# Attention and gated feed-forward in one kernel: load and turn order of batch 1, order of two attention products, and the place of the second scores in chunks 3 to 6

## Chip, cores and metric

The kernel runs on one core of a Trainium2 chip. The metric is the device time of one execution in microseconds (us); the profile is one execution taken by the hardware profiler.

## What is computed

Eight batches of 576 tokens with 8 heads of 64 go through windowed attention. Heads 0 to 3 ("plain") see the last 32 tokens, heads 4 to 7 ("dilated") every fourth of the last 128. The result is the input of a gated feed-forward block.

```python
scores = scale * np.matmul(q, k.transpose(0, 1, 3, 2))
mask_plain = (rel >= 0) & (rel < window)                                      # window 32
mask_dil = (rel >= 0) & (rel < window * dilation) & (rel % dilation == 0)      # dilation 4
attn = np.exp(scores - max); attn = attn / (np.sum(attn) + 1e-09)
x = np.matmul(attn, v)            # turned to (4608 tokens, 512)
g = x @ w_gate                    # 512 x 1536
out = (0.5 * g * (1.0 + erf(g * inv_sqrt2)) * (x @ w_val)) @ w_out   # 1536 x 512
```

## The kernel before

The 4608 tokens are worked through in nine chunks of 512 for the feed-forward part. A chunk c has a gate stage (96 wide matmuls, 128x512, L611: 12 blocks, each with a gate and a value product over 4 parts of the inner dimension) and an out stage (48 wide matmuls, L618: 4 token blocks over 12 parts). Attention of batch c + 1 is put between the wide matmuls of chunk c's out stage; batch 0 comes ahead of the first chunk. The attention result is kept turned in `xT`, four tiles of 128 rows; the dilated heads fill two of them, the plain heads two.

The order is written out by hand. `run_program` reads a string of words: a number n pops n wide matmuls from the stage's list, and a letter with a number n is one step of a pair of heads n. Pairs 4 to 7 are batch 1: 4 and 5 plain, 6 and 7 dilated. In chunk c of the later ones, i and j are the first two pairs of batch c + 1 and k and l the second two. What follows @ is a place in PSUM. The steps are

- t: turn eight rows at a time of q or k on the tensor engine (L366) and copy the result out of PSUM (`turn_first`; pairs 12 and 14 are q, 13 and 15 are k); y: turn rows of nine, q and k together (L386, `turn_second`). The dilated heads of batch 1 use the rows of eight, the plain heads the rows of nine;
- S: scores (L446); P: their exponential on ACT (L476); M: times the mask on VectorE (L481);
- D: sums of the exponentials over the window, by a product with ones (L446, `P,ones` in the profile); l, r: logarithm (L573) and exponential of its negative (L579) on ACT, which give the inverse;
- N: exponentials times the values (L446, `P,v`); X: N times the inverse, on VectorE, into `xT` (L602);
- g, u: gelu on ACT (L770) and its product with the value part on VectorE (L775); w, e: an output block out of PSUM by VectorE (L631) or ACT (L629) and its store; E and G: load of ACT's table for exp/log or for gelu; V: `second` or `second_v`; F, H, R: loads and turns of a later batch.

PSUM has eight banks of 512 fp32; `ps` is one tile over all of them. The instructions of an engine run in the order in which they are written here; waits between engines follow from the data and the banks that they share.

Batch 1 has loads of its own, issued by GpSimd in `second` with a cast to fp16: rows of eight into the unused tails of `xT[2]` and `xT[3]` (72 partitions), rows of nine into `s16` (64 partitions). Ahead of them in GpSimd's queue stand the last gate and value weights (`load_w(3)`), behind them the three pieces of the output weights (`wo`), the masks and batch 1's dilated values. SP's loads of the plain values of batch 1 are held until the first piece of `wo` has landed. For later batches SP loads into `stage`, GpSimd casts, and SP's transposing DMAs turn q and k; the values are cast by GpSimd at L248.

Of the kernel before, what the change touches and what calls it, by code (L numbers as in the profile page):

```python
# [21 lines left out]
def kernel(  # L22
# [11 lines left out]
    B, H, S, D = q.shape  # L34
    NT, DM = out.shape
    DFF = moe_w_gate.shape[1]
    P = 128
# [64 lines left out]
    def eight(b):  # L102

        tails = [xT[2 * b + t][0:R8, 2 * S : 2 * S + HK * 8 * D] for t in range(2)]
        return [t.rearrange("p (h r d) -> p h r d", h=HK, r=8) for t in tails]
# [42 lines left out]
    def load_w(*parts):  # L148

        for i in parts:  # L150
            for t, w in ((wg_t, moe_w_gate), (wv_t, moe_w_val)):
                src = w[:, WC[i][0] : WC[i][1]].rearrange("(kc p) n -> p kc n", p=P)
                nc.gpsimd.dma_start(out=t[i], in_=src)

    def load_wo(i):
        return nc.gpsimd.dma_start(
            out=wo_t[i], in_=moe_w_out[i * CH : (i + 1) * CH, :].rearrange("(fc p) m -> p fc m", p=P)
        )
# [9 lines left out]
    def rows_in(src, r):  # L168

        return src.rearrange("h (p r) d -> p h (r d)", r=r)  # L170

    def load_eights(b, pairs=((0, HK),)):
        for h0, h1 in pairs:
            for t, src in zip(eight(b), (q, k)):
                rows_ = src[b, HK + h0 : HK + h1, :, :].rearrange("h (p r) d -> p h (r d)", r=8)
                nc.gpsimd.dma_start(out=t[:, h0:h1].rearrange("p h r d -> p h (r d)"), in_=rows_)

    def views(b):

        halves = [qraw[b % 2][:, t * QK : (t + 1) * QK] for t in range(2)]  # L180
        qp, kp = (t[:, 0:1280].rearrange("p (g c) -> p g c", g=2) for t in halves)
        qd, kd = (t[:, 1280:QK].rearrange("p (g r i) -> p g r i", g=2, r=4) for t in halves)
        vp, vd = (vraw[b % 3][:, a : a + 2 * NB2 * D].rearrange("p (e d) -> p e d", d=D) for a in (0, 2 * NB2 * D))
        return qp, qd, kp, kd, vp, vd
# [43 lines left out]
    def load_v(b, i, plain):  # L228

        st = st_of(i)  # L230
        for g in range(2 * plain):
            for x in range(2):
                rows_ = v[b, 2 * g + x].rearrange("(j p) d -> p j d", p=64)
                dst = st[half_of(x, b and g), 576 * g : 576 * g + 576].rearrange("p (j d) -> p j d", j=NB2)
                gated(nc.sync.dma_start(out=dst, in_=rows_))  # L235
        for g in range(2 - 2 * plain):
            for x in range(2):
                half = st[half_of(x, g), 576 * g : 576 * g + 512]
                rows_ = v[b, HK + 2 * g + x, 0 : 4 * P].rearrange("(i p r) d -> p i (r d)", i=2, r=4)
                nc.sync.dma_start(out=half.rearrange("p (i c) -> p i c", i=2), in_=rows_)  # L240
        for x in range(2 - 2 * plain):
            dst = st[half_of(x), 512:1152].rearrange("p (g c) -> p g c", c=64)[:, 0:10:9]
            heads = slice(HK + 1, HK + 3) if x else slice(HK, HK + 4, 3)
            nc.sync.dma_start(out=dst, in_=v[b, heads, S - 64 : S].rearrange("g p d -> p g d"))
# [51 lines left out]
    def v_cast(b, g, rest=False):  # L296

        dst = views(b)[5][:, NB2 * g : NB2 * g + NB2]
        for x in range(2):
            half = half_of(x, b and g)  # L300
            nc.gpsimd.dma_start(
                out=dst[half, 0:8].rearrange("p (i r) d -> p i (r d)", r=4),
                in_=v[b, HK + 2 * g + x, 0 : 4 * P].rearrange("(i p r) d -> p i (r d)", i=2, r=4),
            )
            if rest:
                heads = slice(HK + x, H, 2)
                if b:
                    heads = slice(HK + 1, HK + 3) if x else slice(HK, HK + 4, 3)
                nc.gpsimd.dma_start(
                    out=views(b)[5][half_of(x), NB2 - 1 : 2 * NB2 : NB2],  # L310
                    in_=v[b, heads, S - 64 : S].rearrange("g p d -> p g d"),
                )
# [9 lines left out]
    def two_masks():  # L322
        for x in range(2):
            half = slice(64 * x, 64 * x + 64)
            band1 = band[half, 64 * x : 64 * x + BQ]
            nc.gpsimd.tensor_copy(
                two_p[half, 0 : 8 * BQ].rearrange("p (j c) -> p j c", j=8),
                bass.AP(tensor=band1.tensor, offset=band1.offset, ap=[band1.ap[0], [0, 8], [1, BQ]]),
            )
            nc.gpsimd.tensor_copy(two_p[half, 8 * BQ : LP], band1[:, 0:BK])  # L330
        for r in range(4):
            nc.gpsimd.tensor_copy(two_d[:, 176 * r : 176 * r + BQ], two_p[:, 0:BQ])
            nc.gpsimd.tensor_copy(two_d[:, 176 * r + BQ : 176 * r + 176], two_p[:, 0:80])
        rest_mask(nc.gpsimd, two_d[:, LD - BK : LD])
# [339 lines left out]
    for h in range(0, HK, 2):  # L674
        for t, src, eng in ((0, q, nc.sync), (1, k, nc.scalar)):
            first = eng.dma_start(out=first_p[:, t, h : h + 2], in_=rows_in(src[0, h : h + 2], 6))
# [23 lines left out]
    def second():  # L700

        load_w(3)
        load_eights(1)
        for src, t in zip((q, k), nine):
            nc.gpsimd.dma_start(out=t.rearrange("p h r d -> p h (r d)"), in_=rows_in(src[1, 0:HK], 9))
        wo = [load_wo(i) for i in range(3)]
        two_masks()
        v_cast(1, 0, True)
        v_cast(1, 1)
        tiles["two", 1] = views(1)  # L710
        gate["dma"] = wo[0]
        load_v(1, 1, True)
        gate["dma"] = wo[2]
# [84 lines left out]
    def gate_words(c):  # L798

        if c == 0:  # L800
            return (
                "c0@0 c1@0 t0@0@1 t1@1@0 b1@6 W1@3@0 S0@4 P0 t4@0@1 W1@3@0 c2@0 c3@0 t5@1@0 t2@2@1 t3@3@0 D0@40 T0 B0 "
                "t6@1@1 W10@7 t7@0@0 S1@6 P1 b2@2 S2@2 P2 D1@60 T1 B1 b3@0 S3@0 P3 D2@20 A2 N0@40 X0 D3@00 N2@60 X2 A3 N3@20 1 "
                "N1@00 X1 X3 G V 15 g0 u0 g1 u1 4 g2 4 g3 4 u2 4 u3 4 g4 4 g5 4 u4 4 u5 4 g6 4 g7 4 u6 4 u7 4 g8 4 g9 4 u8 3 "
                "t12@4@1 t14@6@0 t13@5@1 t15@7@0 1 u9 8 g10 u10 1 y0@4@5 y1@6@7 7 g11 u11"
            )
        loads = {1: "F3", 2: "R", 3: "F5 H5", 4: "F6 H6", 5: "F7 H7"}.get(c, "")
        rest = " ".join(f"4 g{nb} 4 u{nb}" for nb in range(2, NNB - 1))
        if c == 1:
            return f"{loads} 8 G 3 g0 1 u0 3 g1 1 u1 {rest} 4 g{NNB - 1} 4"  # L810
        before = f"e3@{c - 1}" if c < NCH - 1 else ""
        return f"{before} {loads} 7 G 3 g0 1 u0 1 g1 4 u1 {rest} 4 g{NNB - 1} 4" + (f" u{NNB - 1}" if c > 6 else "")

    def out_words(c):

        if c == 0:
            return (
                "V1 F2 S6@4+S7@6 1 E P6 11 P7 1 M6 S4@4+S5@6 M7 1 P4 6 P5 M4 2 D6@40+D7@60 l6 l7 M5 r6 r7 6 w2@0 4 w1@0 4 "
                "w0@0 H2 D4@52+D5@22 N6@50+N7@20 X6 l5 X7 l4 r4 r5 10 N4@20+N5@40 X4 X5 2 e3@0"
            )  # L820
        if c > 6:
            return "12 e0 12 e1 12 e2 12 w3" if c < NCH - 1 else "12 e0 12 e1 12 e2 L"
        i, j, k, l = (NHP * (c + 1) + n for n in range(NHP))
        first = f"1 u11 4 S{i}@1+S{j}@4 E P{i} P{j} M{i} M{j} 7 w0 5" if c < 3 else f"E P{i} P{j} 1 u11 M{i} M{j} 12 w0 2"
        after = f"S{l + 1}@12+S{l + 2}@15" if 1 < c < 6 else ""
        return (
            f"{first} S{k}@1+S{l}@4 D{i}@11+D{j}@41 P{k} P{l} M{k} M{l} "
            f"{7 if c < 3 else 10} w1 l{i} l{j} r{i} r{j} {10 if c < 3 else 4} N{i}@10+N{j}@40 D{k}@12+D{l}@42 X{i} X{j} "
            f"{2 if c < 3 else 8} w2 {f'l{k} l{l} r{k} r{l}' if c < 3 else f'l{k} r{k} l{l} r{l}'} {8 if c < 3 else 6} N{k}@13+N{l}@43 {after} X{k} X{l} {4 if c < 3 else 5}"
        )  # L830

# [8 lines left out]
    def run_chunk(c):  # L840

        banks = out_banks(c)
        run_program(c, gate_words(c), gate_list(c), banks)
        run_program(c, out_words(c), out_list(c, banks), banks)
# [31 lines left out]
```

## Time and profile before

| | |
|---|---|
| median of 3 runs | 329.22 us (327.46 to 330.02) |
| the profiled execution | 328.32 us |
| its span, first to last instruction | 326.6 us |
| granted TensorE clock | 1.00 |
| instructions | 7737 |
| wide matmuls, L611 and L618 | 1284, mean 0.38 us as recorded |
| GpSimd's software DMA queue | 7.67 MB, 16.7% of 16 engines' span |
| SP's and ACT's DMA queue | 38.29 MB, 50.1% |

PE is the tensor engine, PEld its weight loads, DVE is VectorE, ACT is ScalarE, POOL is GpSimd, SP the engine that issues most DMAs. Busy times are sums of recorded durations; a wide matmul is recorded with 0.38 us, but they overlap, so distances between starts say how fast they follow one another. In a line of the timeline stand start, time from its first start to its last end, engine, line of the kernel, operation, output and inputs, shape and count; in brackets how long the engine had been idle and what ended it. "issue" means that nothing which the profile shows ended the wait.

### The profile page before, as it was taken

To read this page: it belongs to the slowest core of one execution; us is meant where nothing else is said; L and a number is where in the kernel's file an instruction comes from. 1 tells how busy PE (TensorE), PEld (TensorE's weight loads), DVE (VectorE), ACT (ScalarE), POOL (GpSimd) and SP (SyncE) were. 2 spreads that over 40 slices of the span, in tenths; PEclk is the share of its full clock that TensorE was granted. 3 is DMA by queue.
4 is the path that set the end of the run, shared out by engine and by line. 5 is a ranking of instruction groups with operands and counts; after the bars stand their busy time and mean duration, and the time that the engine had idled before them with its cause. 6 is when DMAs were issued, how large, how long until landed. Compare 5 with 4: busy or idle time off the path is not lost.

```text
span 326.6 us, 7737 instructions
## 1 busy us (share of the span) xinstructions
PE 320.2 (98%) x3207; PEld 156.5 (48%) x3207; DVE 151.4 (46%) x226; ACT 159.6 (49%) x240; POOL 82.2 (25%) x134
## 2 busy tenths in 40 slices
PE   7999999999999999999999999999999999999996
PEld 4854545444444454445444454445444544444443
DVE  6854636435643454346533654456334544204320
ACT  2662566435753556346633754366435653233322
POOL 8775603402491422141133301411000000000000
PEclk9999999999999999999999999999999999999999
DMA  8999997998899897798689527972000200020002
GB/s 190 187 201 205 194 200 149 257 190 192 198 242 196 208 197 217 176 223 189 190 202 231 129 97 165 250 173 94 32 2 1 100 33 0 2 96 32 0 34 96
DMA packets 106659, 47.11 MB, mean 144 GB/s; under 512 B 83584, under 2 KB 102144, under 8 KB 106624
## 3 DMA queue, kind: packets, MB, share of 16 engines
q1 hardware_dynamic: 93120, 38.29, 50.1%
q0 software_dynamic: 12944, 7.67, 16.7%
q10 hardware_dynamic: 560, 0.66, 0.7%
q8 instruction: 25, 0.41, 0.5%
q14 instruction: 10, 0.08, 0.1%
HBM read 37.75 MB, written 9.44 MB: 144 GB/s over the span
## 4 chain that ended last, share of the span: by engine, by line
PE 81%; DMA 13%; SPq 2%; ACT 1%; POOL 1%; DVE 1%; issue 0%; POOLq 0%
PE ps L611 50%; PE ps L618 24%; PE ps L446 5%; DMA wo<-in_moe_w_out_dram 5%; DMA wg<-in_moe_w_gate_dram 3%; DMA stage<-in_v_dram 2%; DMA u_all<-in_q_dram 2%; SPq L204 1%; DMA stage<-in_q_dram 1%; PE ps L642 1%; SPq L235 1%; ACT P L476 0%; DVE P L481 0%; POOL s L211 0%; ACT L793 0%
## 5 line engine op out<-in xcount | busy, mean ns | idle before, releaser
L775 DVE SCALAR_TENSOR_TENSOR u_all<-g,ps 128x512 f16<-128x512 f16 x108 | 74.1, 687 | 110.2 <-PE ps L611 93.5
L770 ACT ACTIVATE g<-ps 128x512 f16<-128x512 f32 x108 | 63.6, 597 | 104.1 <-PE ps L611 104.1
L611 PE MATMUL ps<-xT,wg 128*128 128x512 f16 x432 | 112.5, 379 | 0.2
L611 PE MATMUL ps<-xT,wv 128*128 128x512 f16 x432 | 112.4, 379 | 0.0
L618 PE MATMUL ps<-wo,u_all 128*128 128x512 f16 x420 | 96.3, 380 | 0.0
L611 PEld LDWEIGHTS <-wv 128*128 128x128 f16 x432 | 42.2, 98 | 50.9
L611 PEld LDWEIGHTS <-wg 128*128 128x128 f16 x432 | 42.1, 98 | 50.8 <-DMA wg<-in_moe_w_gate_dram 0.2
L618 PEld LDWEIGHTS <-u_all 128*128 128x128 f16 x420 | 39.1, 98 | 45.3 <-issue 0.3
L602 DVE TENSOR_TENSOR xT<-ps,rb 128x576 f16<-128x576 f32 x32 | 28.8, 938 | 16.8 <-PE ps L446 14.0
L476 ACT ACTIVATE P<-ps 128x832 f16<-128x832 f32 (+1 forms) x32 | 25.3, 834 | 15.9 <-PE ps L446 15.8
L211 POOL CAST s<-stage 128x640 f16<-128x640 f32 x24 | 17.0, 735 | 52.0 <-DMA stage<-in_q_dram 37.1
L248 POOL CAST v<-stage 128x1152 f16<-128x1152 f32 x11 | 12.9, 1177 | 61.8 <-DMA stage<-in_v_dram 61.8
L573 ACT ACTIVATE lg<-ps 128x576 f32<-128x576 f32 x30 | 18.7, 653 | 12.7 <-DVE xT L602 9.7
L631 DVE TENSOR_SCALAR osb<-ps 128x512 f32<-128x512 f32 x22 | 15.1, 688 | 12.5 <-PE ps L618 11.6
L579 ACT ACTIVATE rb<-lg 128x576 f32<-128x576 f32 x30 | 19.5, 690 | 0.3
L629 ACT ACTIVATE osb<-ps 128x512 f32<-128x512 f32 x13 | 7.8, 598 | 21.0 <-PE ps L618 21.0
L223 POOL CAST s<-stage 128x512 f16<-128x512 f32 x24 | 14.4, 627 | 10.7 <-DMA stage<-in_q_dram 7.5
L481 DVE TENSOR_TENSOR P<-P,two_p 128x832 f16<-128x832 f16 x14 | 10.0, 722 | 10.1 <-ACT P L476 10.1
L481 DVE TENSOR_TENSOR P<-P,two_d 128x768 f16<-128x768 f16 x14 | 8.9, 639 | 8.9 <-ACT P L476 8.1
L795 ACT ACT_TABLE_LOAD x9 | 11.5, 1283 | 0.2
L446 PE MATMUL ps<-q 64*64 64x96 f16 (+2 forms) x576 | 10.0, 202 | 0.7 <-issue 0.4
L446 PEld LDWEIGHTS <-v 64*64 64x64 f16 x616 | 7.9, 107 | 5.8 <-issue 4.7
(67 smaller groups left out, 134.7 us busy)
## 6 DMA issues: line engine op xcount, KB each, us to landing
out_dram<-osb SPq DMA_DIRECT2D x35, 256.0 KB, 2.3
stage<-in_v_dram SPq DMA_DIRECT2D x28, 144.0 KB, 3.8
stage<-in_q_dram SPq DMA_DIRECT2D x24, 128.0 KB, 3.3
stage<-in_k_dram SPq DMA_DIRECT2D x24, 128.0 KB, 3.1
stage<-in_q_dram SPq DMA_DIRECT2D x6, 512.0 KB
stage<-in_k_dram SPq DMA_DIRECT2D x6, 512.0 KB, 5.3
stage<-in_v_dram SPq DMA_DIRECT2D x20, 128.0 KB, 2.9
wo<-in_moe_w_out_dram POOLq DMA_DIRECT2D x3, 512.0 KB, 16.1
```

The costliest lines, as they stand in the source:

```text
L211: nc.gpsimd.tensor_copy(s16[:, 1280 * t + 640 * g : 1280 * t + 640 * g + 640].rearrange("p (k c) -> p k c", k=5), st_of(i).rearrange("p (k ...
L446: nc.tensor.matmul(o[cols], lhs[rows], rhs[rows], start=st, stop=end, skip_group_check=True)
L476: nc.scalar.activation(pt[:, 0 : src.shape[1]], src, AF.Exp, bias=0.0, scale=scale)
L481: nc.vector.tensor_tensor(pt, pt, mask, ALU.mult)
L573: nc.scalar.activation(lg, psf[:, c0 : c0 + S], AF.Ln)
L579: nc.scalar.activation(rb, tiles.pop(("lg", n)), AF.Exp, scale=-1.0)
L602: nc.vector.tensor_tensor(dst, num, rb, ALU.mult)
L611: nc.tensor.matmul(ps[:, bank, :], w[:, kc, ns], xT[kc][:, tok], start=first, stop=end)
L618: nc.tensor.matmul(ps[:, bank, :], u_all[:, fc, tb * P : (tb + 1) * P], wo_t[fc // 4][:, fc % 4, :], start=(fc == 0), stop=(fc == NNB - 1),)
L631: nc.vector.tensor_scalar(osb, ps[:, bank, :], 1.0 / USCALE, None, ALU.mult)
L770: nc.scalar.activation(g, ps[:, gate_banks(c, args[0])[0], :], AF.Gelu)
L775: nc.vector.scalar_tensor_tensor(u_all[:, nb, :], tiles.pop(("g", nb)), USCALE, val, ALU.mult, ALU.mult)
```

## The change

In `second` the two loads of rows of nine are issued ahead of the two of rows of eight. In the gate words of chunk 0 the turns `y` take the place of the four `t`, and the four `t` that of the `y`. In the out words of chunk 0, N6 and N7 come ahead of D4 and D5. In the out words of chunks 3 to 6 one wide matmul more stands ahead of the second scores (S of k and l) and of the D of i and j, and one less between them and `w1`.

```diff
@@ second
         load_w(3)
-        load_eights(1)
         for src, t in zip((q, k), nine):
             nc.gpsimd.dma_start(out=t.rearrange("p h r d -> p h (r d)"), in_=rows_in(src[1, 0:HK], 9))
+        load_eights(1)
         wo = [load_wo(i) for i in range(3)]
@@ gate_words, chunk 0, last line
-                "t12@4@1 t14@6@0 t13@5@1 t15@7@0 1 u9 8 g10 u10 1 y0@4@5 y1@6@7 7 g11 u11"
+                "y0@4@5 y1@6@7 1 u9 8 g10 u10 1 t12@4@1 t14@6@0 t13@5@1 t15@7@0 7 g11 u11"
@@ out_words, chunk 0, last line
-                "w0@0 H2 D4@52+D5@22 N6@50+N7@20 X6 l5 X7 l4 r4 r5 10 N4@20+N5@40 X4 X5 2 e3@0"
+                "w0@0 H2 N6@50+N7@20 D4@52+D5@22 X6 l5 X7 l4 r4 r5 10 N4@20+N5@40 X4 X5 2 e3@0"
@@ out_words, later chunks
-        first = f"1 u11 4 S{i}@1+S{j}@4 E P{i} P{j} M{i} M{j} 7 w0 5" if c < 3 else f"E P{i} P{j} 1 u11 M{i} M{j} 12 w0 2"
+        first = f"1 u11 4 S{i}@1+S{j}@4 E P{i} P{j} M{i} M{j} 7 w0 5" if c < 3 else f"E P{i} P{j} 1 u11 M{i} M{j} 12 w0 3"
             f"{first} S{k}@1+S{l}@4 D{i}@11+D{j}@41 P{k} P{l} M{k} M{l} "
-            f"{7 if c < 3 else 10} w1 l{i} l{j} r{i} r{j} {10 if c < 3 else 4} N{i}@10+N{j}@40 D{k}@12+D{l}@42 X{i} X{j} "
+            f"{7 if c < 3 else 9} w1 l{i} l{j} r{i} r{j} {10 if c < 3 else 4} N{i}@10+N{j}@40 D{k}@12+D{l}@42 X{i} X{j} "
```

## The prediction

> **What bounds the kernel now.** I read the page's busy shares first, then the chain that ended last, then what TensorE (PE) waited for, then the timeline around each edited place.
>
> ```profile
> PE 320.2 (98%) x3207; PEld 156.5 (48%) x3207; DVE 151.4 (46%) x226; ACT 159.6 (49%) x240; POOL 82.2 (25%) x134
> PE 81%; DMA 13%; SPq 2%; ACT 1%; POOL 1%; DVE 1%; issue 0%; POOLq 0%
> ```
>
> PE is busy for 98% of the span and carries the chain; no other engine passes 49%. So the order of work matters only where it makes PE stand. The waits of PE, whole span, give these (total us, times, longest):
>
> ```profile
> PE ps L659 <- DVE ones L67: 1.5, 1, 1.5
> PE ps L446 <- DVE P L481: 0.6, 1, 0.6
> PE ps L446 <- issue: 0.4, 1, 0.4
> ```
>
> The first is the start. The other two, with one stand too short for this list, lie beside the edits. I use starts of instructions, since a matmul's end is modelled: 96 wide matmuls took 20.72 us in the chain (55.70 to 76.42), 0.216 us each.
>
> Timeline, all engines, around batch 1:
>
> ```profile
> 35.33 1.23 PE L366 MATMUL ps<-ident,xT 72*64 72x72 f16 x64
> 38.76 0.85 PE L386 MATMUL ps<-ident,s 64*64 64x64 f16 x72
> 41.16 0.51 PE L446 MATMUL ps<-q 64*64 64x96 f16 x32
> 42.09 0.22 PE L446 MATMUL ps<-q 64*64 64x64 f16 x4 [0.43 <-issue]
> 51.30 0.57 PE L446 MATMUL ps<-P,ones 64*64 64x64 f16 x20
> 51.70 0.52 PE L446 MATMUL ps<-P,v 64*64 64x96 f16 x40
> 52.36 2.16 DVE L602 TENSOR_TENSOR xT<-ps,rb 128x576 f16<-128x576 f32 x2 [0.26 <-PE ps L446]
> 52.70 0.65 ACT L573 ACTIVATE lg<-ps 128x576 f32<-128x576 f32 x1 [2.07 <-issue]
> 54.57 0.58 PE L446 MATMUL ps<-P,v 64*64 64x96 f16 x40
> ```
>
> L366 at 35.33 turns the rows of eight, L386 at 38.76 the rows of nine. The last four matmuls of the scores S6, S7 come at 42.09 instead of near 41.5: PE stands 0.6 us by starts, and the view names no releaser. Plain values N4, N5 start at 54.57. Ten wide matmuls (2.16 us) run from 52.16, and a change from wide to small ones costs another 0.09 (from 7 wide ones before 41.16: 1.5 us from 39.54 plus 0.1), so 54.41 was due: 0.16 is lost, and they start as the two X (L602) end, 52.36 + 2.16 = 54.52.
>
> The four loads (us from issue to landing), and GpSimd's first and last issue of them:
>
> ```profile
> xT<-in_q_dram POOLq DMA_DIRECT2D x1, 288.0 KB, 14.6
> xT<-in_k_dram POOLq DMA_DIRECT2D x1, 288.0 KB, 14.1
> s<-in_q_dram POOLq DMA_DIRECT2D x1, 288.0 KB, 14.7
> s<-in_k_dram POOLq DMA_DIRECT2D x1, 288.0 KB, 15.8
> ```
>
> ```profile
> 20.09 0.76 POOL L176 DMA_DIRECT2D xT<-in_q_dram  x1
> 22.18 0.64 POOL L705 DMA_DIRECT2D s<-in_k_dram  x1
> ```
>
> Eights (xT) land at 34.7 and 34.9, nines (s) at 36.25 and 38.0. Both are there before PE turns them.
>
> Chunk 4, and chunk 5 beside it:
>
> ```profile
> 182.80 0.54 PE L446 MATMUL ps<-q 64*64 64x96 f16 x36
> 183.98 0.57 PE L446 MATMUL ps<-P,ones 64*64 64x96 f16 x26 [0.60 <-DVE P L481]
> 217.65 0.54 PE L446 MATMUL ps<-q 64*64 64x96 f16 x36
> 218.01 0.56 PE L446 MATMUL ps<-P,ones 64*64 64x96 f16 x28
> 182.37 1.56 DVE L481 TENSOR_TENSOR P<-P,two_p 128x832 f16<-128x832 f16 x1 [0.16 <-ACT P L476]
> 182.34 1.15 POOL L248 CAST v<-stage 128x1152 f16<-128x1152 f32 x1 [7.80 <-DMA stage<-in_v_dram]
> ```
>
> In chunk 5 the sums D start 0.36 us after the scores S; in chunk 4 1.18 us after, so 0.82 are lost. The mask product M (L481) took 1.56 us there against 0.59 for the one before it (181.61), beside a GpSimd cast that began 0.03 us earlier.
>
> **What the skill says.** "GPSIMD Engine Reference", section "Key points": GpSimd shares its SBUF interfaces with VectorE and they contend when a VectorE instruction has two SBUF inputs. M has two; the trace agrees (1.56 against 0.59). "PSUM — Partial Sum Buffer", section "PSUM bank collisions raise a hardware error": engines have to be kept apart by bank, not by address, two readers included. The trace agrees in its order: Ln of D4, which shares bank 6 with N6, starts at 53.58 after X6. "DMA: Bandwidth & Descriptors", section "Queues, rings and completion order": each DMA engine takes descriptors in ring order; the four landings above come in the order of issue.
>
> **Part A, loads swapped.** Four issues stay four: GpSimd spends 2.7 us on them in either order, and the three wo loads, the masks and batch 1's value loads queue behind as before. One of those value loads, at 38.22, waited for the last nine to land; it would wait for the last eight, at the same time. SP's next load is held until the first wo has landed. The first output load wo lands at 24.32 + 16.1 = 40.4, 2.4 us after the last nine, and the two nines land 1.7 us apart. The transfer ahead, val weights, issued at 19.36 with 12.3 to landing, lands at 31.6. So two nines from there, 1.7 each, land at 33.3 and 35.0; the eights take the rest and end at about 38.0, as the nines do now. What is behind the four keeps its place.
>
> **Part B, turns swapped.** The 64 + 72 transposes and the wide matmuls between remain. Nines turn at 35.33: both q and k must be there, so cover is 0.3 us. From the turn of nines to the next wide one is 0.78 us (38.76 to 39.54), of eights 1.16 (35.33 to 36.49); the eights therefore start at 36.11 + 2.27 = 38.38, with 0.4 us cover behind a landing at 38.0, and end where the nines do now, 39.54. Seven wide matmuls later S6, S7 are due at 41.15, as before. The copies now in front of them: ACT 1.30 us from 38.87, VectorE 2 x 0.75 + 0.21 from 39.1, ended by 40.8: 0.35 us to spare. These copies end when those of the nines end now (39.32 + 1.41 = 40.73), so gelu 11 behind them on ACT is not later. The stand at 42.09 has no named cause, so I leave it: 0, with ends of -0.6 (it goes) and +0.6 (twice as long).
>
> **Part C, dilated values N6, N7 ahead of D4, D5.** Same 60 matmuls in one block; PE gains nothing by itself. X6 can begin when N6 is done and D4 has left bank 6, near 52.1 and not 52.36. But X7 shares bank 3 with D5, and the Ln of D5 stands ahead of it. That Ln began 0.35 us after X6 did, although both waited for the same block. If it starts at once after D5, X7 ends 0.2 earlier and the 0.16 at N4 go; if it keeps its delay and D5 ends 0.1 later (its last products are wide), X7 starts near 53.5 instead of 53.4 and N4 loses 0.1 to 0.15 more. Ends -0.16 and +0.15; I take 0.
>
> **Part D, S one wide matmul later in chunks 3 to 6.** Nothing is added: 15 and 10 become 16 and 9. D follows S, so M gets 0.216 us more. In chunks 3, 5 and 6 PE does not stand at D, gain 0. In chunk 4, 0.216 of the 0.82 go. Behind it in chunk 5: ACT's two exponentials, two Ln and two inverses move by 0.2; the last ended at 222.24 and X began at 222.66, so they stay hidden. Ends: 0 if the cast no longer meets M, and in that case 0.8 go by themselves. I take -0.2.
>
> **Sum.** 0 + 0 + 0 - 0.2 = -0.2 us. The profiled execution took 328.32 us, its span 326.6 and 1.7 around it, so 328.1. That execution is 0.9 under the median of the runs shown, 329.22; against it the forecast is 329.0.
>
> **Rivals.**
> 1. Gain: N4's stand goes (-0.16), the unnamed one at 42.09 too (-0.6), and the cast misses M (-0.8): 329.22 - 1.6 = 327.6. For it: all three are in the trace. Against: A and B don't touch what is queued in front of S6, and the cast missed M by chance elsewhere. Chance 0.2.
> 2. Slower: the nines land late and PE stands at their turn at 35.33, with all behind it waiting. It decides from a landing of nine k after 35.3. If its bytes move no sooner than half of the 3 us that I reckon, it lands at 36.5: +1.2, less 0.2 by D, 330.2. The upper end is today's landing, 38.0: +2.65 - 0.2, 331.7. For it: 0.3 us of cover is little beside 1.7 between landings. Against: ring order, and equal bytes in front. Chance 0.25.
> 3. C turns against itself by 0.15 and D meets no collision: 329.4. Chance 0.1. My forecast keeps 0.45.
>
> **Numbers.** The runs shown go from 327.46 to 330.02, wider than any of these terms; 1% (3.3 us) is about what can be told from no change. Range 327.4 to 330.6: rivals 1 and 2 and this spread. Chances: to be faster by over 1%, all stands together don't suffice (1.6 us), 0.04; slower by over 1% needs more than today's landing of the nines, or something unseen, 0.07; within, 0.89.
>
> **What would show it.** Right: nine k lands near 35.0 and L386 starts near 35.33 with no wait, L366 near 38.4, S6 near 41.15, D in chunks 3 to 6 about 0.36 us after S, or 0.6 longer than that where a cast meets M. X6 starts near 52.1. Wrong: PE waits for DMA at L386 or L366, S6 waits for a copy, or N4 starts later than 54.6. A change of more than 2 us in either direction would mean that PE stood somewhere I did not look, and would refute this.

## The result, and the profile after

| | before | after |
|---|---|---|
| median, us | 328.05 (327.46 to 330.02, 17 runs) | 327.13 (326.76 to 327.77, 17 runs) |
| ratio on record, all runs [95% interval] | | 0.9968 [0.9957, 0.9979] |
| the profiled execution, us | 328.32 | 327.72 |
| its span, us | 326.6 | 326.0 |

By medians the change gains 0.92 us, 0.28%; the ratio on record puts it at 0.32%. It was forecast to stay within 1%, and it does, but 327.13 lies 0.27 under the lower end of the range. The median of 329.22, on which the forecast stood, came from three runs; more runs of the same kernel put it at 328.05.

The busy shares and the waits of PE after (total us, times, longest):

```profile
PE 320.4 (98%) x3207; PEld 156.5 (48%) x3207; DVE 150.3 (46%) x226; ACT 159.6 (49%) x240; POOL 82.2 (25%) x134
PE ps L446 <- DVE P L481: 0.3, 1, 0.3
```

PE is still the bound, with the same 3207 matmuls. What changed is how long it stands. The wait for the mask product in chunk 4 went from 0.6 to 0.3; the wait put down to "issue" (0.4 before) is no longer in PE's list.

Batch 1 in the timeline after:

```profile
35.38 0.85 PE L386 MATMUL ps<-ident,s 64*64 64x64 f16 x72
38.43 1.23 PE L366 MATMUL ps<-ident,xT 72*64 72x72 f16 x64
41.21 0.86 PE L446 MATMUL ps<-q 64*64 64x96 f16 x36
41.84 0.11 PEld L446 LDWEIGHTS <-q 64*64 64x64 f16 x3 [0.23 <-issue]
51.05 0.55 PE L446 MATMUL ps<-P,v 64*64 64x96 f16 x40
51.81 2.17 DVE L602 TENSOR_TENSOR xT<-ps,rb 128x576 f16<-128x576 f32 x2
54.19 0.58 PE L446 MATMUL ps<-P,v 64*64 64x96 f16 x40
```

The nines turn at 35.38 without a wait, the eights at 38.43, S6 and S7 start at 41.21: up to here PE is 0.05 later than before. All 36 score matmuls are now in one group of 0.86 us, where 32 ran ahead of the stand before. Three of the weight loads still wait, until 41.84: a stand of 0.29 by starts instead of 0.59. The values N6, N7 come first (51.05), the two X run in one piece from 51.81, 0.76 after the block's start and not 1.06; N4 starts at 54.19. That is where it was due: ten wide matmuls from 51.93 take 2.16, and the change to small ones 0.09. Its loss of 0.16 is gone.

Of the four loads, nine k and eight k, us from issue to landing:

```profile
s<-in_k_dram POOLq DMA_DIRECT2D x1, 288.0 KB, 13.9
xT<-in_k_dram POOLq DMA_DIRECT2D x1, 288.0 KB, 14.9
```

The four, issued at 20.30, 20.91, 21.51 and 22.26, land at 33.3, 34.8, 35.4 and 37.1. The last of the four landed at 38.0 before: all four together end 0.9 sooner, and the first output load behind them lands at 39.65 instead of 40.4.

Chunk 4:

```profile
182.69 0.54 PE L446 MATMUL ps<-q 64*64 64x96 f16 x36
183.57 0.57 PE L446 MATMUL ps<-P,ones 64*64 64x96 f16 x26 [0.31 <-DVE P L481]
182.04 1.48 DVE L481 TENSOR_TENSOR P<-P,two_p 128x832 f16<-128x832 f16 x1 [0.16 <-ACT P L476]
181.93 1.15 POOL L248 CAST v<-stage 128x1152 f16<-128x1152 f32 x1 [7.69 <-DMA stage<-in_v_dram]
```

The cast still meets M (1.48 us for M). The first two products of D run early in both kernels; the other 26 start 0.88 after the scores S instead of 1.18.

Between the two profiled executions: +0.05 up to the turns, -0.30 in S6/S7, -0.13 from the start of the block of N and D to N4, -0.3 in chunk 4, and a small rest of +0.1. That is the -0.6 of the span. The medians differ by 0.92.

### The profile page after: what moved, and what is told of

It reads as the page before. It is cut to its first block, busy times and chain, and to the rows that moved or that the text cites. A ratio compares the mean times of both kernels' runs of the same rounds, so it can differ in the third digit from the quotient of the medians.

```text
span 326.0 us, 7737 instructions
## 1 busy us (share of the span) xinstructions
PE 320.4 (98%) x3207; PEld 156.5 (48%) x3207; DVE 150.3 (46%) x226; ACT 159.6 (49%) x240; POOL 82.2 (25%) x134
## 4 chain that ended last, share of the span: by engine, by line
PE 92%; DMA 2%; POOL 2%; ACT 1%; DVE 1%; issue 0%
PE ps L611 57%; PE ps L618 28%; PE ps L446 6%; DMA wg<-in_moe_w_gate_dram 2%; POOL xT L176 1%; PE ps L642 1%; POOL v L301 1%; ACT P L476 0%; DVE P L481 0%; ACT L793 0%; POOL v L309 0%; PE ps L366 0%; PE ps L386 0%; POOL band L117 0%; ACT g L770 0%
## 5 line engine op out<-in xcount | busy, mean ns | idle before, releaser
L618 PEld LDWEIGHTS <-u_all 128*128 128x128 f16 x420 | 39.1, 98 | 45.5 <-issue 0.5
L446 PEld LDWEIGHTS <-q 64*64 64x64 f16 x576 | 7.9, 107 | 5.1 <-issue 3.2
```

The lines of the kernel that those rows point to most:

```text
L446: nc.tensor.matmul(o[cols], lhs[rows], rhs[rows], start=st, stop=end, skip_group_check=True)
L618: nc.tensor.matmul(ps[:, bank, :], u_all[:, fc, tb * P : (tb + 1) * P], wo_t[fc // 4][:, fc % 4, :], start=(fc == 0), stop=(fc == NNB - 1),)
```

## The experiments

A is the loads swapped, B the turns swapped, C the values ahead of the sums, D the later second scores. Ratios, with their 95% intervals, are to the kernel before. Its median was 328.27 beside the first four experiments, 328.21 beside the next four, 328.07 beside the last four.

**A and B alone.** The swaps in `second` and in `gate_words`, on the kernel before.

> Parts A and B alone on the kernel before. Theory 1 (the stand of PE inside the scores S6, S7 is a wait for PE's own instructions, which come in blocks by DMA; B makes PE begin its block about 0.4 us sooner, so the next one is asked for sooner): the four last score matmuls come about 0.3 us after the thirty-two instead of 0.6, N4 keeps its 0.16, chunk 4 keeps a stand of 0.8 when a cast meets M. About -0.3 us. Theory 2 (the stand belongs to the gelu product u11, that ended 0.06 us ahead of it in the kernel before, or is chance): the stand stays 0.6, time unchanged.

327.26 us, 0.9976 [0.9966, 0.9986], span 325.2.

```profile
41.19 0.55 PE L446 MATMUL ps<-q 64*64 64x96 f16 x36
```

The 36 scores run in one piece of 0.55 us, with no stand, where a stand of 0.3 was expected. N4 (54.00) is still 0.16 late, and in this execution no cast met M in chunk 4, which is 0.8 of the 1.4 that the span is shorter by. By medians A and B bring 1.0 us, the whole change 0.92; the intervals don't tell the two apart.

**C alone.**

> Part C alone on the kernel before. Theory 1: X6 begins about 0.75 us after the block of D and N instead of 1.06, the Ln of D5 about 1.05 instead of 1.40, N4 has no stand: -0.15 us, and the stands in S6 and chunk 4 stay as in the kernel before. Theory 2 (the gain at N4 came from the earlier parts): N4 still starts 0.16 us late and nothing changes.

328.04 us, 0.9994 [0.9981, 1.0007]: no effect that can be measured.

```profile
38.78 1.18 PE L386 MATMUL ps<-ident,s 64*64 64x64 f16 x72
53.58 1.15 DVE L602 TENSOR_TENSOR xT<-ps,rb 128x576 f16<-128x576 f32 x1 [0.21 <-ACT lg L573]
```

Two things are in these lines. The first X starts early, as after, but the second waits 0.21 for the logarithm of D5, and N4 is 0.11 late. And the turn of nines, in its old late place, takes 1.18 instead of 0.85: in this execution nine k landed at 39.08 and PE stood 0.31 within it. With the old order the nines' landing is not safe either.

**D alone.**

> Part D alone on the kernel before. Theory 1: a chunk whose M is met by a cast stands 0.2 us less (0.8 to 0.6 in chunk 4), the others not at all: -0.2 us. Theory 2 (D also acts in the unprofiled runs in chunks 3, 5 and 6, where a cast may meet M in other executions): more than -0.4 us in the median while the profile shows 0.2.

328.31 us, 1.0007 [0.9993, 1.002]. In its profile no cast met M in chunk 4, so D had nothing to take away; S6/S7 stood 0.39. So this profile can't tell what D is worth; the interval leaves room for a gain of 0.2 at most.

**What PE waits for at S6/S7.** The view names no releaser. The page has a queue that the prediction didn't use, q8:

```profile
q8 instruction: 25, 0.41, 0.5%
```

These are 25 packets of 16 KB. PE has 2 x 3207 = 6414 instructions (weight loads and matmuls), about 256 to a packet. Counted in order of their starts, PE stands behind instruction 1217 in both kernels, at the 33rd score matmul of S6/S7. If blocks of 256 end there, they end at 961, 705, 449 and 193 too (call these places edges), and up to 6414 there are 25 edges, as many as packets. The Trainium skill, "Runtime: NRT & Kernel Launch", section "Instruction fetch mechanics", says that an engine's instructions are refilled in 16 KiB blocks of 256 by a DMA queue of the engine's sequencer, at a cost that is "mostly hidden". The size agrees with the trace; whether it is hidden here was the question. So the edge was moved by the number of PE's small warming matmuls at the kernel's start, and nothing else was changed.

Eight fewer (16 instructions), with nearly the same total of columns (2196, not 2208):

```diff
-    warm(69, 7, 32, 32)
+    warm(61, 7, 32, 36)
```

> The kernel before with 61 warming matmuls of 36 columns instead of 69 of 32: the same columns, 16 PE instructions fewer ahead of everything. Theory 1 (wait for a block of 256 instructions): the stand after the thirty-second score matmul goes, since the edge of the block now lies 16 instructions later, among the wide matmuls, about 1 us later: S6 and S7 in one piece, at most 0.1 us of stand a few wide matmuls later, about -0.5 us. Theory 2 (data, banks or u11): the stand stays behind the thirty-second score matmul with 0.6 us, time unchanged.

327.77 us, 0.9985 [0.9974, 0.9997], span 325.8. The scores run in one piece (`x36` at 41.69), as the wait for a block wants it; but another stand is now three edges earlier, between score matmuls of batch 0:

```profile
13.94 0.40 PE L446 MATMUL ps<-q 64*64 64x96 f16 x12 [0.28 <-issue]
```

That one is 0.44 us long, behind instruction 449 = 1217 - 3 x 256. The median is 0.5 lower than before, with an interval that ends just under 1, which speaks for the stand in the other runs too.

Eight more (2156 columns):

```diff
-    warm(69, 7, 32, 32)
+    warm(77, 7, 32, 28)
```

> The kernel before with 77 warming matmuls of 28 columns instead of 69 of 32: 16 PE instructions more ahead of everything. Theory 1 (edge of a block of instructions): the stand is now behind the twenty-fourth score matmul of S6, S7, eight sooner, with 0.4 to 0.8 us. Theory 2 (data, banks): it stays behind the thirty-second.

328.71 us for the one execution, span 327.0.

```profile
41.50 0.44 PE L446 MATMUL ps<-q 64*64 64x96 f16 x24
42.46 0.29 PE L446 MATMUL ps<-q 64*64 64x80 f16 x12 [0.52 <-issue]
```

The stand has moved eight matmuls ahead, from behind the 32nd to behind the 24th, as 16 more instructions want. No data and no bank of the scores changed between these kernels. PE stands at S6/S7 for its own next block of instructions.

When the block comes is then read from the trace. PE crosses the edge ahead of it (instruction 961) during the turns. Before, that edge is late in the turn of eights, at 36.27; after, the dense turn of nines has it at 35.85 (144 instructions in 0.78 us against 128 in 1.16). The next packet of q8, in windows of 0.5 us from 39.7 before and from 39.2 after:

```profile
q8 instruction: 1, 0.02, 12.2%
q8 instruction: 1, 0.02, 11.2%
```

It follows 3.5 us after the edge in both: at 39.79 before, 39.33 after, and ends at 40.76 and 40.22. The 33rd score matmul goes at 42.10 and 41.84. From edge to edge PE has 5.2 us of work before and 5.7 after. Where PE stood in S6/S7, over all profiles, it went on 5.6 to 6.1 us after the edge. So the new order has just about the time that a block needs, and the old one doesn't.

**B without A.** Turns swapped, loads in the old order.

> Part B without part A: the rows of nine are turned at 35.35 us while their loads still stand behind those of the rows of eight. Theory 1 (the swap of the loads is what gives the turn its cover): PE stands at the turn of the nines until nine k lands, 37.9 to 39.1 in the kernels with the old order, so 2.6 to 3.7 us; behind it the block of instructions is asked for sooner against its use and the stand in S6, S7 goes. In all +2 to +3.2 us. Theory 2 (cover is wide anyway): no stand, time as with A and B, -0.8.

333.0 us, 1.0139 [1.0117, 1.0162], span 331.1: slower by 4.8, more than either theory had.

```profile
37.22 0.22 PE L386 MATMUL ps<-ident,s 64*64 64x64 f16 x2 [1.77 <-DMA s<-in_q_dram]
38.95 0.93 PE L386 MATMUL ps<-ident,s 64*64 64x64 f16 x70 [1.51 <-DMA s<-in_k_dram]
40.22 1.91 PE L611 MATMUL ps<-xT,wg 128*128 128x512 f16 x4
```

PE stands 3.5 us for the two nines. Behind that, seven wide matmuls follow one another at about 0.425 us instead of 0.216 (the third line: four in 1.70), 1.5 us more; the granted clock between 40 and 42 us was 0.50. The two make 5.0; the stand in S6/S7 (0.6) is gone, and the span is 4.5 longer. So B needs A; the second rival, slower by late nines, is real where A is missing.

**C with an ACT instruction more.** C alone as above, and one small ACT copy at the start of the kernel.

```diff
+    scr1 = const.tile([P, 1], F16, tag="scr1")
+    nc.scalar.copy(scr1, ones[:, 0:1])
```

> Part C on the kernel before, with one instruction more on ACT at the start (a copy of one column). In part C alone the Ln of D5 began 0.38 us after PE's signal, as in every kernel with the old turns; with A and B, which have one waiting instruction fewer on ACT, 0.07. Theory 1 (the lag hangs on where that Ln lies in ACT's stream of instructions, not on data): the Ln begins about 0.07 us after the signal, X7 no longer waits for it, and N4 has no stand: -0.1 to -0.2 us against part C alone. Theory 2 (the lag comes from the loads or from the order of the copies): it stays 0.38 and N4 stands 0.1 late.

328.03 us, 0.9998 [0.9984, 1.0011].

```profile
52.26 2.16 DVE L602 TENSOR_TENSOR xT<-ps,rb 128x576 f16<-128x576 f32 x2
52.60 0.65 ACT L573 ACTIVATE lg<-ps 128x576 f32<-128x576 f32 x1 [1.71 <-issue]
```

The logarithm starts 0.3 earlier than with C alone (52.90), the two X run in one piece, N4 has no stand. The median, 328.03 against 328.04 for C alone, is too coarse for the 0.1. Counted with its waits and DMA issues, ACT has 63 instructions ahead of this logarithm before and with C alone, 62 after and with A and B alone, and here 64. It is late with 63 and on time with 62 and 64. So in the change it is B that lets this logarithm start at once, and C that lets the first X start early; with A and B alone N4 was still late. Why 63 is late is not shown.

**D with the collision forced.** In chunk 6, where nothing met M, a GpSimd cast of 128 x 1152 is held behind the first M of the pair, once on the kernel before, once on the one after (the diff is an excerpt: it leaves out the cast's two tiles, and `last_m`, which holds the last M):

```diff
-        first = ... P{i} P{j} 1 u11 M{i} M{j} 12 ...
+        first = ... P{i} P{j} 1 u11 M{i} J M{j} 12 ...
+            elif kind == "J":
+                cast = nc.gpsimd.tensor_copy(scr16, scr32)
+                tc.add_manual_dep(cast.ins, tiles["last_m"].ins.name, SYNC, ...)
```

> The kernel before with one more GpSimd cast (128x1152, of the size of L248's) in chunk 6 that starts when the first mask product of that chunk is done, so that it runs ahead of and beside the second. Theory 1: that second mask product takes 1.2 to 1.6 us instead of 0.59, and PE stands 0.5 to 0.8 us at the sums of chunk 6, where it does not stand in the kernel before. Theory 2 (the long product in chunk 4 has another cause): 0.59 and no stand.

> The same cast in the changed kernel. Theory 1: the mask product is as long as in the kernel before with the cast, and the stand at the sums of chunk 6 is one wide matmul, 0.216 us, shorter. Theory 2: it is as long.

328.76 (span 327.1) and 327.62 us (span 325.9) for one execution each. M and D on before, then on after (lines are two further down):

```profile
250.90 1.49 DVE L483 TENSOR_TENSOR P<-P,two_p 128x832 f16<-128x832 f16 x1 [0.16 <-ACT P L478]
252.44 0.57 PE L448 MATMUL ps<-P,ones 64*64 64x96 f16 x26 [0.53 <-DVE P L483]
```

```profile
249.98 1.49 DVE L483 TENSOR_TENSOR P<-P,two_p 128x832 f16<-128x832 f16 x1 [0.16 <-ACT P L478]
251.52 0.57 PE L448 MATMUL ps<-P,ones 64*64 64x96 f16 x26 [0.32 <-DVE P L483]
```

M takes 1.49 in both. The stand, which follows D's first two matmuls, is 0.70 before and 0.48 after: 0.22 less, one wide matmul (0.216). So the cast makes M long, and D takes one wide matmul off the stand.

**A version beyond both.** Three kernels on top of the kernel after, which was not run again beside them. The first has 61 warming matmuls and holds batch 6's value casts (in `load_rest`) until both M of chunk 4 are done (an excerpt; the word K stands behind these M):

```diff
-        if not by_pool:
+        if not by_pool and b != 6:
...
+            elif kind == "K":
+                first = cast_v(views(6)[5], 2)
+                tc.add_manual_dep(first.ins, tiles["last_m"].ins.name, SYNC, ...)
+                cast_v(views(6)[4], 1)
```

> The changed kernel with 16 PE instructions fewer at the start (61 warming matmuls of 36 columns) and with batch 6's casts of the values held until the second mask product of chunk 4 is done. Theory 1: no stand in S6, S7 (0.3 in the changed kernel), none at the sums of chunk 4 (0.5 there): the span ends 0.3 to 0.8 us sooner than in the changed kernel's profile, near 325.3, and the median lies 0.2 to 0.5 under it. Theory 2 (these stands are not in most executions): the median stays at the changed kernel's, 327.1.

327.35 us, 0.9976 [0.9965, 0.9987]: no stand in S6/S7 or chunk 4, but a new one of 0.67 at 14.23 at the earlier edge. No gain on after. The second leaves the casts and moves the edge later, by eight small matmuls fewer from 11 us on:

```diff
-                "t6@1@1 W10@7 t7@0@0 ...
+                "t6@1@1 W2@7 t7@0@0 ...
```

> The changed kernel with 8 of the 10 filling matmuls ahead of the eighth turn of batch 0 taken out, 16 PE instructions fewer from there on. The first edge of a block of 256 PE rows stays where it is (row 193), all later ones fall 16 rows later in the program. Theory 1: no new stand near 14 us (the kernels with 16 fewer from the very start had one of 0.4 to 0.7 there), and none in S6, S7: span 0 to 0.3 us under the changed kernel's. Theory 2 (the filling matmuls are needed to keep PE going): the start of the wide matmuls moves back by 0.5 us or more.

327.14 us, 0.9963 [0.995, 0.9975], span 325.6. The scores run in one piece (`x36` at 41.22, 0.54 us), and no stand appears elsewhere at an edge; chunk 4 still stands 0.54, and the median is that of the kernel after, 327.13. Both together, `W2` and the held casts:

> The same and batch 6's casts of the values held until the second mask product of chunk 4 is done. Theory 1: no stand in S6, S7, none at the sums of chunk 4; span near 325.2 and 0.3 to 0.8 us under the changed kernel's profile; the median 0.1 to 0.4 under its 327.1. Theory 2: the median stays at 327.1 because these stands are short in most executions.

326.95 us, 0.996 [0.9943, 0.9978], span 324.9.

```profile
181.39 0.59 DVE L481 TENSOR_TENSOR P<-P,two_p 128x832 f16<-128x832 f16 x1 [0.16 <-ACT P L476]
182.04 1.15 POOL L248 CAST v<-stage 128x1152 f16<-128x1152 f32 x1 [8.63 <-DVE P L481]
182.40 0.56 PE L446 MATMUL ps<-P,ones 64*64 64x96 f16 x28
```

M is back at 0.59, D follows S (182.04) after 0.36. This is the fastest kernel of the study, 1.1 us under before; its 0.18 under after are less than the intervals can tell.

**All profiles together.** The stands differ from one execution to the next, so one pair of profiles says little about the median. By starts, in us:

| stand of PE | old order | new order |
|---|---|---|
| S6/S7, edges unmoved | before 0.59, C 0.48, D 0.39, C with ACT 0.67, cast on before 0.85 | after 0.29, A and B 0, cast on after 0 |
| turn of nines (turns old or new) | C 0.3, none in six others | none in six |
| N4 (D first or N first) | 0.15 to 0.17, 0.28 with 16 fewer | C alone 0.11, else none |
| chunk 4 (without and with D) | 0.72 to 0.84 in three of eight | 0.53 and 0.54 in two of four |

B alone is left out of the second row, and held casts of the last. The turns of batch 1 start between 35.1 and 36.2. Take that start, these stands and those of the forced casts from the spans, and 289.7 to 289.8 us are left in every kernel but B alone, where PE ran at half pace. So behind the start of the turns nothing else moves these profiles by more than 0.1. An estimate of what the change is worth, from this table: 0.50 by S6/S7, 0.15 by N4, 0.05 by the nines, and 0.1 by chunk 4 (0.22 to 0.3 where a cast meets M, in 5 of 12). That is 0.8 of the median's 0.92, and within the interval of the ratio, 0.7 to 1.4 us. It would also explain why the `W2` kernel gained nothing on after: in two of three profiles of the new order S6/S7 had no stand left to remove.

## Why the prediction was wrong

**The level.** The forecast set its -0.2 against 329.22, though the profiled execution lay 0.9 under it. The later median of the kernel before was 328.05. This is the larger part of the miss, 1.17 of 1.87: -0.2 on that level would be 327.85. The range hung on the same three runs; its lower end is rival 1, reckoned from 329.22. And it left out rival 2's own upper end, 331.7. That the change stayed within 1% says little, since all known stands together were half of that.

**Part A: the nines right, the cost right, one figure off.** Nine k was put at 35.0 and landed at 34.8; no wait at L386. "They end at about 38.0" was wrong: 37.1, and the first output load 0.75 sooner. No stand of PE hung on it.

**Part B: the failed step.** "The stand at 42.09 has no named cause, so I leave it: 0." It had a cause, PE's next instruction block, and B touches it: the edge ahead of it lies in the turns, and with the nines there PE crosses it 0.42 sooner. The sentence against rival 1, "A and B don't touch what is queued in front of S6", fails with it. The term is -0.30 in the profile after, half of the -0.6 that the working kept as its lower end, -0.6 with A and B alone, and about -0.5 by all profiles. Every time in this part (turn at 38.38, S6 at 41.15) was right within 0.06.

**Part C: 0 taken, -0.13 measured.** The working named the right condition: whether the logarithm of D5 starts at once. It did, 0.07 after PE's signal, against 0.38 before. What was missing is that B decides it.

**Part D: the mechanism right, the price that of one execution.** -0.2 was taken in chunk 4 and 0 in the others. The forced collision gives 0.22. In the profile of after, chunk 4 gained 0.3; M was also 0.08 shorter there, so not all of it is D's. Where the cast misses M, as with D alone, it is 0. That the cast met M in both profiles, before and after, is chance: it did so in five of the twelve kernels that leave it free, so D is worth about 0.1 in the mean.

**The rivals.** Rival 1 had the direction: N4's stand went and that in S6/S7 was halved, but the cast still met M, so 0.6 in the profiles, 0.9 in the medians, and not 1.6. Its 327.6 is near 327.13 by luck: it was reckoned from 329.22, and from 328.05 it would be 326.5. Rival 2 was excluded by A, and B without A shows its mechanism at a higher price than the 1.2 to 2.65 reckoned. Rival 3 is refuted for the profiled execution: C did not turn against itself, and the cast met M.

**What stays open.** The estimate of 0.8 rests on one profile for each kernel and few of each kind; how often each stand comes in other executions is not measured. A alone was not run. That B and not A shortens the stand in S6/S7 rests on the trace: the packet comes 3.4 to 3.6 us after the edge in either order of the loads, and it is the edge that comes sooner. The packet that ended at 40.22 let PE go on at 41.84 after the change, and by 41.53 at the latest with A and B alone; the difference was not found. That the ACT logarithm's 0.3 also comes from a block's edge, of ACT's own instructions, is not shown.

## What to carry to other kernels

A stand of the bounding engine for which the profile names no releaser should be checked against the engine's instruction count. If such stands lie a multiple of 256 instructions apart, and move when a few small instructions are added far ahead of them, the engine waits for its own instructions, and code order and density between the edges are what can be tuned. Many small matmuls between two edges are the risky place: here 256 instructions in 5.2 us, where the same number takes 27.6 us of wide matmuls alone. And the level of a forecast should come from the profiled execution and many runs; three runs were 1.2 us off, more than the whole effect.

## What the runs showed of the hardware

- PE's instructions come in 16 KB packets, 25 for 6414 instructions. At S6/S7 the packet started 3.2 to 3.6 us after the edge in all kernels, took 0.9 to 1.05, and PE went on 1.3 to 1.6 us after its end where it stood. Elsewhere in the profile before, packets started from 4.2 us ahead of the instruction at the edge to 4.9 behind it, so these 3.5 us are of this stretch, and why they are so many was not isolated.
- After 3.5 us of standing in two pieces PE ran seven wide matmuls at half its pace, with a granted clock of 0.50. The Trainium skill, "TensorE: Matmul & The Clock Gate", section "Part 1: The HAM clock gate (the "warmup" mystery)", gives 426.7 ns between starts at N = 512 for a cold array and 215.7 for a warm one, and an idle window of about 3.4 us; the run agrees with 0.427 and 0.216. The window was not measured here.
- A GpSimd cast beside a mask product with two SBUF inputs stretched it from 0.59 to between 1.45 and 1.58 us in five kernels, and to 1.49 where the cast was forced to meet it.
- The order of the four loads changes when all four have landed, for the same bytes: with the nines first at 36.9 to 37.3 in six kernels, with the eights first at 37.9 to 39.1 in eight.
